# An attention-and-MLP kernel on one core: a planner's order is replaced by a fixed table, with the first weights and the first layer's pieces laid out anew

## The chip, the cores and the metric

The kernel runs on one core of a Trainium2 chip. The metric is the device time of one launch in microseconds (us). One core has five engines that run their own instruction streams in order: TensorE (PE, matmuls), VectorE (DVE), ScalarE (ACT), GpSimd (POOL) and SyncE (SP, which here only issues transfers). ACT and POOL issue transfers too.

## The reference

```python
# q, k, v: (4 batches, 8 heads, 768 steps, 64), f32
gamma = 1.0 - 2.0 ** (-5.0 - np.arange(H))
for t in range(S):
    state = gamma * state + einsum('bhd,bhe->bhde', k[:, :, t], v[:, :, t])
    y[:, :, t] = scale * einsum('bhd,bhde->bhe', q[:, :, t], state)
x = y.transpose(0, 2, 1, 3).reshape(3072, 512)
h = x @ w_in                       # 512 -> 2048
g = 0.5 * h * (1 + tanh(c * (h + 0.044715 * h**3)))
out = g @ w_out                    # 2048 -> 512
```

A linear attention with a decay for each head gives x, and a two-layer MLP with a tanh-gelu follows. All matmuls run in f16 with f32 sums.

## The kernel before

**Tiling.** The 768 steps are cut into six chunks c = 0 to 5 of 128 steps. A chunk has 4 batches of 128 steps, which are 512 tokens for the MLP. For each chunk and batch the attention does these steps on PE, with a helper for each (lines of the kernel before, and behind the slash those of the kernel after):

- T (`mm_T`, L211/L268): 8 transposes turn q and k (f16) into `qkT`. From chunk 3 on q is transposed in another way and T has 4 matmuls.
- A (`mm_A`, L220/L277): 16 matmuls on 64x64 tiles of the array, the products of k and q inside the chunk. DVE multiplies them by the decay mask (`ev_A1`, two evictions of 0.68 us for a batch).
- yc (`mm_yc`, L239/L296): the part of y from the state of earlier chunks, two batches at a time, on 64x64 tiles.
- Y (`mm_yi`, L251/L308): 8 matmuls on 128x64 tiles, the part of y from inside the chunk. The eviction gives x of this batch in f16.
- S (`mm_s`, L262/L319): 8 matmuls on 128x64 tiles for a batch, the update of the state.

The MLP's first layer is M1, its second M2. Chunk 0 and 1 have M1 as plain matmuls (`moe1_mm`, L357/L414), chunk 0 has M2 so (`m2_mm`, L515). All other chunks have both layers as 7 products of half-size blocks (`m1w_mm`, L492; `m2w_mm`, L504), whose sums DVE and POOL form (`tt`, L394) and whose results ACT (`copy_on`, L159) and DVE collect from PSUM in `st` and `o` tiles.

**Transfers.** A row is one of q, k, v of one chunk and batch, 256 KB of f32. The rows of chunk 0 are issued on SP and ACT. The weights come in 8 blocks of 512 KB, `w_in` 0 to 3 (`load_w_in`, L338) and `w_out` 0 to 3 (`load_w_out`, L347), issued on POOL. A cast on POOL, DVE or ACT makes f16 of each row (`cast`, L176 with a scale, L159 or L161 plain).

**Order.** All instructions are issued in the order in which the program emits them; each engine then runs its own in that order and waits for what it needs. Chunk 0 is written out by hand (L531 to L601): `spin(n)` puts n matmuls on zeros where PE would wait (32 in all), T, A, Y and S of the four batches follow one another, M1 of chunk 0 begins with `moe1_two` on feature pairs 0 to 2 in pieces of 256 and 128 tokens, and goes on with `moe1` for the features 6 to 15, 512 tokens wide. On POOL the casts of k and q of batches 2 and 3 stand between the issues of the weights:

```python
    load_w_in(0)
    prep1(PO, "k", 0, 2)
    for i in range(1, 4):
        load_w_in(i)
    prep1(PO, "k", 0, 3)
    prep1(PO, "q", 0, 3)
    for i in range(NO):
        load_w_out(i)
```

The loads of chunk 1 are held back by a one-element copy on ACT behind a gelu of chunk 0 (L608). Everything else, M2 of chunk 0 included, is ordered by a list scheduler while the program is built. It has a cost for each kind of step and engine (`KIND`), times at which engines, buffers and transfers come free, four threads of PE work, and takes the unit that can start first. Its units for PE keep pairs together: A of two batches, yc with both Y, S of two batches.

Of the kernel before, what the change touches and what calls it, by code (L numbers as in the profile page):

```python
# [12 lines left out]
ALU = mybir.AluOpType  # L13


@with_exitstack
def kernel(
# [9 lines left out]
    nc = tc.nc  # L27
    B, H, S, Dh = q.shape
# [92 lines left out]
    load1(nc.sync, "k", 0, 2)  # L121
    load1(nc.sync, "q", 0, 3)
    load1(nc.sync, "v", 0, 3)

# [7 lines left out]
    def spin(n):  # L132
        ps = bank("h", shape=(128, 512), name="spin_ps")
        for _ in range(n):
            nc.tensor.matmul(
                out=ps, lhsT=zero[:, 0:128], rhs=zero, start=True, stop=True
            )
# [180 lines left out]
    def o_S(b, tag="att"):  # L318
        pss["S", b] = bank(tag, shape=(128, NHP, 64), name="s_ps")  # L319
        mm_s(0, b, pss["S", b])  # L320

    def o_evS(b, eng=nc.vector):
        copy_on(eng, st_of(b), pss.pop(("S", b)))


# [48 lines left out]

    def moe1(c, fc):
        h_ps = bank("h", shape=(128, B * C), name="h_ps")
        moe1_mm(c, fc, h_ps, 0, B * C)
        gelu(g_tile(c, fc)[:, fc % 2], h_ps)

    def moe1_two(c, fp, t0, t1):  # L380

        h_ps = bank("h", shape=(128, 2, B * C // 2), name="h_ps")
        for r in range(2):
            moe1_mm(c, 2 * fp + r, h_ps[:, r, 0:t1 - t0], t0, t1)
        gelu(g_tile(c, 2 * fp)[:, :, t0:t1], h_ps[:, :, 0:t1 - t0])
# [145 lines left out]
    load1(AC, "q", 0, 2)  # L531
    load1(AC, "v", 0, 2)
# [6 lines left out]
    load1(AC, "k", 0, 3)  # L539
# [10 lines left out]
    o_S(0, "o")  # L550
    o_evY(0, AC)
    prep1(VE, "q", 0, 2)

    load_w_in(0)
    prep1(PO, "k", 0, 2)
    for i in range(1, 4):
        load_w_in(i)
    prep1(PO, "k", 0, 3)
    prep1(PO, "q", 0, 3)
    for i in range(NO):  # L560
        load_w_out(i)
    o_A(1)
    o_evA(1)
    spin(3)
    o_T(2)
    o_evT(2, AC)
    spin(2)
    o_Y(1)
    o_S(1, "o")
    o_evY(1, AC)  # L570
    prep1(AC, "v", 0, 2)
    spin(2)
    o_A(2)
    o_evA(2)
    o_evS(0, AC)
    prep1(AC, "v", 0, 3)
    o_evS(1, AC)
    spin(6)
    o_T(3)
    o_evT(3)  # L580


    t01, t2, t3 = (0, half), (half, half + C), (half + C, 2 * half)
    moe1_two(0, 0, *t01)
    o_A(3)
    o_evA(3)
    o_Y(2)
    o_S(2)
    o_evY(2, AC)
    moe1_two(0, 1, *t01)  # L590
    o_evS(2)
    moe1_two(0, 0, *t2)
    moe1_two(0, 1, *t2)
    o_Y(3)
    o_S(3)
    o_evY(3)
    o_evS(3)
    moe1_two(0, 2, *t01)
    for fp in range(2):
        moe1_two(0, fp, *t3)  # L600
    moe1_two(0, 2, half, 2 * half)  # L601

    raw["q", 1, 0] = tile_of(*LD1[0], shape=SIZE["ld"][1])
    ld_at["q", 1, 0] = LD1.pop(0)
    for fc in range(6, NF):
        moe1(0, fc)
        if fc == 12:
            nc.scalar.copy(out=raw["q", 1, 0][0:1, 0, 0:1], in_=g_tile(0, 10)[0:1, 0, 0:1])  # L608
    for bs in ((0, 1), (2, 3)):
        for b in bs:  # L610
            load1(SY, "q", 1, b)
            load1(SY, "k", 1, b)
        for b in bs:
            load1(SY, "v", 1, b)
    nc.sync.dma_start(out=dec.rearrange("p h t -> p (h t)"), in_=dec_h.ap())

    ENG = {"ACT": AC, "DVE": VE, "POOL": PO, "SP": SY}
    KIND = {
        "gelu": {"ACT": (0.51, 0.60)},
        "snap": {"ACT": (0.51, 0.59)},  # L620
        "add": {"DVE": (0.62, 0.70)},
        "evA": {"DVE": (0.61, 0.69)},
        "evY": {"DVE": (0.61, 0.69)},
        "evY1": {"ACT": (0.51, 0.59), "DVE": (0.61, 0.69)},
        "evS": {"DVE": (1.10, 1.20)},
        "evT": {"DVE": (0.62, 0.69), "ACT": (0.92, 1.01)},
        "cast": {"ACT": (0.53, 0.62), "POOL": (0.58, 0.62)},
        "cast2": {"ACT": (1.06, 1.15), "POOL": (1.18, 1.22)},
        "trq": {"DVE": (0.60, 0.69)},
        "evTk": {"DVE": (0.36, 0.44), "ACT": (0.50, 0.58)},  # L630
        "loadq": {"SP": (8.6, 0.0)},
        "scale": {"POOL": (1.00, 1.05), "DVE": (0.68, 0.75)},
        "scale1": {"POOL": (1.00, 1.05), "DVE": (0.68, 0.75)},
        "sumg": {"POOL": (1.12, 1.16), "DVE": (0.35, 0.42)},
        "sumx": {"POOL": (1.12, 1.16)},
        "sumw": {"DVE": (0.35, 0.42)},
        "sume": {"POOL": (1.12, 1.16), "DVE": (0.35, 0.42)},
        "load": {"SP": (0.90, 0.0)},
        "store": {"SP": (0.80, 0.0)},
    }  # L640
    LAT_PE, LAT, SAFE, AHEAD = 0.28, 0.07, 1.5, 0.4
    tok, T = {}, {}
    slots = {p: [0.0] * n for p, (n, _, _) in SIZE.items()}
    slots["bank"] = [0.0] * 8
    held_by = {}
    free_at = {"PE": 34.2, "ACT": 34.7, "DVE": 25.0, "POOL": 21.0, "SP": 47.5}
    landed = [48.6, 49.6, 51.5, 52.4]
    port = [0.0]
    todo, by_need = [], {}

    class Op:
        def __init__(self, kind, emit, needs, gives, alloc=(), free=(), slack=1.0, early=(), kb=0):
            self.kind, self.emit, self.needs, self.gives = kind, emit, needs, gives
            self.alloc, self.free, self.slack, self.early, self.kb = alloc, free, slack, early, kb

    def shared(o, e):

        return e == "POOL" or e == "DVE" and o.kind[:3] in ("sum", "sca")

    def op(*a, **k):  # L660
        todo.append(Op(*a, **k))

    def when(needs):
        t = 0.0
        for n in needs:
            if n not in tok:
                return None
            t = max(t, tok[n])
        return t

    def room(alloc):

        t, seen = 0.0, {}
        for off, (key, *_) in alloc:
            seen.setdefault(key[0], []).append(off)
        for p, offs in seen.items():
            at = sorted(x for x in slots[p] if x is not None)
            if len(at) < len(offs):
                return None
            t = max(t, max(a - o for a, o in zip(at, sorted(offs))))  # L680
        return t

    def take(alloc):
        for key, readers, *shape in alloc:
            p = key[0]
            i = min((x, i) for i, x in enumerate(slots[p]) if x is not None)[1]
            if p == "lq" and key[2] in BLK:
                i = key[3]
            slots[p][i] = None
            held_by[key] = [p, i, readers, 0.0]  # L690
            T[key] = bank_tile(i, *shape) if p == "bank" else tile_of(p, i)

    def give_back(keys, t):
        for key in keys:
            h = held_by[key]
            h[2] -= 1
            h[3] = max(h[3], t)
            if h[2] == 0:
                slots[h[0]][h[1]] = h[3]

    def finish_op(o, e, s):
        busy, lat = KIND[o.kind][e]
        free_at[e] = s + busy
        end = s + lat + LAT
        if shared(o, e):
            port[0] = s + busy
        if e == "SP":
            begin = max(landed[-1], s + 1.3)
            landed.append(max(begin + 1.15 * o.kb / 256, s + busy + 1.8 if o.kind == "loadq" else 0.0))
            end = landed[-1] + SAFE  # L710
            free_at[e] = max(free_at[e], landed[-4] if o.kind == "load" else 0.0)
        take(o.alloc)
        o.emit(ENG[e])
        for n in o.early:
            tok[n] = s
        for n in o.gives:
            tok[n] = end
        give_back(o.free, end)


    def ld_key(c, b, nm):
        early = c == 2 and b < 2 and nm != "v" or c in BLK and nm == "q"
        return ("lq" if early else "ld", nm, c, b)

    def q_cast(c, b):
        key = ("qk16", c, b)

        def emit(eng):
# [8 lines left out]
           alloc=[(key, 2 if c + 1 == NCk else 3)], early=[("al", key)], free=[("lq", "q", c, b)], slack=2.0)  # L737

        def tr(eng):
# [7 lines left out]
           early=[("al", "qkT", c, b)], free=[key], slack=1.5)  # L747

    def q_load(c):
# [3 lines left out]
        def emit(eng):  # L753
# [8 lines left out]
           early=[("issued", key)], slack=3.0, kb=1024)  # L762
        prev[0] = ("issued", key)

    def cast_in(c, b, nm):
# [4 lines left out]
        ldk = ld_key(c, b, nm) if c > 1 else ("ld", nm, c, b)  # L770
# [8 lines left out]
        if nm == "v":  # L779
            kind = "cast" if c < 2 else "scale"  # L780
        elif kind == "scale":
            kind = "scale1"
# [7 lines left out]
            slack=8.0 if nm == "v" else 2.0,  # L790
        )

    prev = [None]

    def load_in(c, b, nm):
# [3 lines left out]
        def emit(eng):  # L799
            eng.dma_start(  # L800
                out=T[ldk], in_=srcs[nm][b, :, c * C:(c + 1) * C, :].rearrange("h p d -> p h d")
            )

        op("load", emit, [prev[0]] if prev[0] else [], [key], alloc=[(ldk, 1)],
           early=[("issued", key)], slack=3.0, kb=256)
        prev[0] = ("issued", key)

    def sub(cost, emit, needs=(), gives=(), alloc=(), free=()):
# [504 lines left out]
```

## Time and profile before

| | |
|---|---|
| median of 3 runs | 204.56 us (204.36 to 206.03) |
| the profiled execution | 204.52 us |
| its span, first to last instruction | 202.7 us |
| mean granted TensorE clock | 0.998 |
| PE busy | 192.5 us, 95% of the span, 2376 matmuls |
| DVE / ACT / POOL busy | 150.5 / 126.6 / 96.6 us |
| DMA moved | 30.1 MB |
| first M1 matmul of chunk 0 | 17.87 us |
| last matmul ends, last store lands | 199.69, 201.83 us |

A line of a timeline gives start, duration, engine, line, operation, the tiles out<-in, their shapes, the count, and in brackets the idle time before it with what ended it. A line of the waits gives total us, times, and the longest. In a table of windows each engine has its busy us and, in brackets, its instructions; then follow the granted clock, the DMA share and GB/s.

### The profile page before, as it was taken

The numbers are of one execution on the slowest core, as the hardware profiler recorded it, in microseconds if no ns is written. First come the engines' busy times: TensorE is split into PE (matmuls) and PEld (weight loads), VectorE is DVE, ScalarE is ACT, GpSimd is POOL, SyncE is SP. The second block draws the span as 40 slices with busy tenths as digits, with TensorE's granted clock in tenths as the row PEclk, the third lists the DMA queues.
The fourth block names the chain that finished last, engine by engine and source line by source line (L and its number), as shares of the span: only waits on it lengthen the run. The fifth ranks groups of instructions, "written<-read, shape, count | busy, mean of one in ns | idle before, by whom it ended". The sixth has DMA issues, their size and how long they took to land. (4 is left out here: it accounts for less than half of the span.)

```text
span 202.7 us, 5761 instructions
## 1 busy us (share of the span) xinstructions
PE 192.5 (95%) x2376; PEld 153.1 (76%) x2376; DVE 150.5 (74%) x283; ACT 126.6 (62%) x235; POOL 96.6 (48%) x96
## 2 busy tenths in 40 slices
PE   7769999999999997999999999999999999999993
PEld 3336744455898885889889878789888888888883
DVE  4435585739787998997799998799995793297720
ACT  2482466053589547749948849948859916499421
POOL 0697000011202876852999903498914799241400
PEclk9999999999999999999999999999999999999999
DMA  7999999989998799968990669990002300020205
GB/s 165 287 263 206 209 204 218 224 196 247 206 229 169 116 251 217 224 109 152 250 254 12 117 98 188 228 259 2 3 0 84 127 3 3 0 103 25 83 4 204
DMA packets 95898, 30.10 MB, mean 148 GB/s; under 512 B 88320, under 2 KB 92800, under 8 KB 95872
## 3 DMA queue, kind: packets, MB, share of 16 engines
q1 hardware_dynamic: 85120, 23.45, 49.7%
q0 software_dynamic: 4224, 4.19, 12.5%
q10 hardware_dynamic: 6528, 2.10, 4.1%
q8 instruction: 18, 0.29, 0.6%
q14 instruction: 8, 0.07, 0.1%
HBM read 27.64 MB, written 6.29 MB: 167 GB/s over the span
## 5 line engine op out<-in xcount | busy, mean ns | idle before, releaser
L394 DVE TENSOR_TENSOR st<-ps,st 128x512 f32<-128x512 f32 x48 | 31.3, 681 | 9.4 <-PE ps L492 3.6
L504 PEld LDWEIGHTS <-s_g 128*128 128x128 f16 x320 | 30.8, 98 | 5.1 <-DVE s_g L394 0.8
L159 ACT COPY st<-ps 128x512 f32<-128x512 f32 x48 | 26.4, 602 | 13.0 <-PE ps L492 12.8
L373 ACT ACTIVATE g<-st 128x512 f16<-128x512 f32 x48 | 29.9, 649 | 7.3 <-DVE st L394 7.3
L492 PEld LDWEIGHTS <-w_in 128*128 128x128 f16 x256 | 24.7, 98 | 3.9 <-issue 0.6
L271 DVE TENSOR_TENSOR a<-ps,mask 128x512 f16<-128x512 f32 x40 | 24.8, 680 | 3.3 <-PE ps L220 3.3
L357 PEld LDWEIGHTS <-w_in 128*128 128x128 f16 x232 | 20.8, 98 | 7.7 <-issue 0.7
L394 POOL TENSOR_TENSOR s_g<-g 128x512 f16<-128x512 f16 x17 | 19.9, 1184 | 13.9 <-ACT g L373 13.9
L394 POOL TENSOR_TENSOR s_g<-g,s_g 128x512 f16<-128x512 f16 x15 | 17.8, 1191 | 16.2 <-DVE s_g L394 16.1
L159 ACT COPY o<-ps 128x512 f32<-128x512 f32 (+1 forms) x28 | 14.8, 529 | 17.0 <-PE ps L504 14.1
L504 PEld LDWEIGHTS <-g 128*128 128x128 f16 x240 | 23.1, 98 | 3.0
L373 ACT ACTIVATE g<-ps 128x512 f16<-128x512 f32 x32 | 19.3, 602 | 5.6 <-PE ps L357 5.4
L492 PEld LDWEIGHTS <-u_w 128*128 128x128 f16 x192 | 18.5, 98 | 3.0 <-issue 0.6
L504 PE MATMUL ps<-t_w,s_g 128*128 128x256 f16 x160 | 18.9, 273 | 1.2 <-ACT o L159 0.7
L504 PE MATMUL ps<-w_out,s_g 128*128 128x256 f16 x160 | 19.6, 273 | 0.0
L504 PE MATMUL ps<-w_out,g 128*128 128x256 f16 x160 | 19.3, 273 | 0.0
L492 PE MATMUL ps<-xs,w_in 128*128 128x256 f16 x128 | 18.6, 273 | 0.4 <-DVE st L394 0.4
L394 POOL TENSOR_TENSOR s_g<-s_g,g 128x512 f16<-128x512 f16 x10 | 11.9, 1187 | 14.8 <-DVE s_g L394 14.7
L394 DVE TENSOR_TENSOR o<-ps,o 128x512 f32<-128x512 f32 (+1 forms) x18 | 10.7, 593 | 9.6 <-PE ps L504 9.6
L492 PE MATMUL ps<-xs,u_w 128*128 128x256 f16 x128 | 16.6, 273 | 0.5 <-DVE a L271 0.5
L492 PE MATMUL ps<-x,w_in 128*128 128x256 f16 x128 | 16.3, 273 | 0.0
L357 PE MATMUL ps<-x,w_in 128*128 128x256 f16 x128 | 15.3, 273 | 0.1
(73 smaller groups left out, 320.6 us busy)
## 6 DMA issues: line engine op xcount, KB each, us to landing
ld<-in_v_dram SPq DMA_DIRECT2D x19, 256.0 KB, 4.4
ld<-in_k_dram SPq DMA_DIRECT2D x17, 256.0 KB, 5.3
out_dram<-o SPq DMA_DIRECT2D x8, 512.0 KB, 3.8
ldq<-in_q_dram SPq DMA_DIRECT2D x48, 64.0 KB, 2.8
w_in<-in_moe_w_in_dram POOLq DMA_DIRECT2D x4, 512.0 KB, 9.4
w_out<-in_moe_w_out_dram POOLq DMA_DIRECT2D x4, 512.0 KB, 14.4
ld<-in_q_dram SPq DMA_DIRECT2D x5, 256.0 KB, 4.6
out_dram<-o SPq DMA_DIRECT2D x5, 256.0 KB, 3.0
```

Of the source, the lines that this page charges most:

```text
L159: eng.copy(out=out, in_=in_)
L271: eng.tensor_tensor(out=a_sb[c, b, j], in0=ps, in1=mask[:, j], op=ALU.mult)
L357: nc.tensor.matmul(out=out, lhsT=w_in_sb[wi][:, kc, wr * 128:(wr + 1) * 128], rhs=xT[c][:, kc, t0:t1], start=(kc == 0), stop=(kc == NHP - ...
L373: nc.scalar.activation(out=out, in_=in_, func=AF.Gelu_apprx_tanh, scale=1.0)
L394: eng.tensor_tensor(out=out, in0=in0, in1=in1, op=op)
L492: nc.tensor.matmul(out=ps[:, f], lhsT=m1_lhs(lk, kc, 2 * g + f), rhs=x[:, kc], start=(n in FIRST and kc == 0 and f == 0), stop=(n in (1, 5 ...
L504: nc.tensor.matmul(out=ps, lhsT=m2_lhs(c, lk, fp, a), rhs=m2_rhs(rk, fp), start=(first and fp == 0), stop=(n in (1, 5, 6) and fp == NP - 1 ...
```

## The change

The planner and the written-out order of chunk 0 behind Y of batch 1 are taken out. In their place stands `ORDER`, a table of some 950 words. A word is an engine's letter (p PE, a ACT, v DVE, g POOL, s SP) and an item's number; w2 means 2 spins. The items are the same small steps as before, and the program emits them in the order of the table. With it come these changes:

- A and Y are items of one batch each, so the table can set them apart; S of chunk 0 is an item for each batch, with its eviction on ACT.
- `w_in` part 0 is issued on POOL behind a one-element copy from q of batch 0, before the casts of k; part 1 follows the casts of k of batches 0 and 1. The table then begins with the issues of `w_in` 2, 3 and `w_out` 0, 1, 2 (g0 to g4), then the casts of v of batches 2 and 3 on POOL (g9, g12), then `w_out` 3 (g5) and a one-element copy (g6, `hold`) behind which SP's loads of chunk 1 may start.
- The casts of q and k of batches 2 and 3 are on DVE, those of v on POOL. The rows of batches 2 and 3 are issued on SP, but for q of batch 2, which ACT issues.
- M1 of chunk 0 has 24 pieces: 8 feature pairs for batches 0 and 1 (256 tokens), for batch 2 (128) and for batch 3 (128). M2 of chunk 0 waits for the pieces that it reads.
- The load of the decay table `dec` goes behind q and k of chunk 2.
- The spins are 14, 3, 2, 3, 5 by hand and twice 2 in the table: 31.

```diff
+ORDER = """
+v7 p180 v8 g0 w2 p192 p170 g1 g2 g3 g4 g9 g12 g5 g6 v169 s13 s14 s15 s16 v10 p194 p186 a179
+a191 p173 v171 p182 a193 a181 w2 p196 s17 g27 s18 s19 v172 s20 s21 g30 s22 p184 s23 s24 a195
...
+"""
...
-    load1(nc.sync, "k", 0, 2)
-    load1(nc.sync, "q", 0, 3)
-    load1(nc.sync, "v", 0, 3)
+    load1(nc.scalar, "q", 0, 2)
+    for at in (("k", 2), ("v", 2), ("q", 3), ("k", 3), ("v", 3)):
+        load1(nc.sync, at[0], 0, at[1])
...
+    nc.gpsimd.tensor_copy(out=w_in_sb[0][0:1, 0, 0:1], in_=raw["q", 0, 0][0:1, 0, 0:1])
+    load_w_in(0)
     spin(14)
...
     o_Y(0)
-    o_S(0, "o")
     o_evY(0, AC)
...
+    def m1_first():
+        for t0, t1, bs, cost, kind in ((0, half, (0, 1), 0.873, "gelu"), (half, half + C, (2,), 0.45, "gelu2"),
+                                       (half + C, 2 * half, (3,), 0.45, "gelu2")):
+            for fp in range(NP):
...
+                def emit(fp=fp, t0=t0, t1=t1, key=key):
+                    for r in range(2):
+                        moe1_mm(0, 2 * fp + r, T[key][:, r, 0:t1 - t0], t0, t1)
...
+    for b in range(2):
+        tok["x", 0, b] = (12.0, 14.2)[b]
...
+            tok[key] = ((10.4, 13.9, 14.9), (15.8, 19.4, 20.4))[b - 2][i]
...
+    load_w_in(1)
+    for n in range(2, 8):
+        trig("win" if n < 4 else "wout", n % 4, n)
+    hold()
...
+    for at, word in enumerate(ORDER.split()):
+        e, i = word[0], int(word[1:])
+        if e == "w":
+            ps = bank_tile(min(x for x in slots["bank"] if x is not None)[1], (128, 512), name="spin_ps")
+            spin_on(ps, i)
+            continue
+        o = items.pop(i)
+        take(o.alloc)
+        o.emit(by[e])
...
+        give_back(o.free, 1000.0 + at)
```

`trig` issues one block of weights, each after the one before it. The numbers in `tok` are times at which rows are taken to have landed (q, k, v of batch 2: 10.4, 13.9, 14.9; of batch 3: 15.8, 19.4, 20.4). In this program they order nothing; the table alone does.

The order on PE behind Y of batch 1 begins: S of batch 0, 2 spins, M1 of batches 0 and 1 on feature pair 0, T of batch 2, M1 pair 1, S and A of batch 2 and S of batch 1, 2 spins, M1 pair 2, Y of batch 2, M1 pair 3, T of batch 3, M1 of batch 2 on pairs 0 to 2, S of batch 3, M1 of batch 2 on pair 3, A of batch 3, then M1 from pair 4 on.

## The prediction

> **What bounds the kernel now.** I read the windows of busy time first, to see where TensorE (PE) is not full, then PE's waits, then PE's timeline at the head, then the queues of POOL and SP there. The profiled execution took 204.52 us (span 202.7, so 1.8 lie outside it), 0.04 under the median of 204.56; all sums are made against 204.5.
>
> ```profile
> core 0: us, PE busy (x) PEld busy (x) DVE busy (x) ACT busy (x) POOL busy (x), PEclk, DMA share, GB/s
> 5.00:10.00 5.00, 3.80 (x45) 1.83 (x45) 2.10 (x4) 1.98 (x3) 3.16 (x3) 1.00 1.27 287
> 10.00:15.00 5.00, 3.22 (x62) 2.05 (x61) 1.76 (x3) 4.30 (x9) 4.43 (x6) 1.00 1.28 265
> 15.00:20.00 5.00, 4.80 (x75) 2.98 (x74) 2.67 (x5) 1.30 (x4) 3.88 (x5) 1.00 1.24 207
> 20.00:25.00 5.00, 4.52 (x67) 3.94 (x65) 2.97 (x9) 2.58 (x7) 0.00 (x0) 1.00 1.24 206
> 25.00:30.00 5.00, 5.00 (x28) 2.46 (x27) 4.29 (x12) 3.18 (x7) 0.00 (x0) 1.00 1.24 206
> 70.00:80.00 10.00, 9.16 (x132) 7.74 (x130) 9.14 (x14) 5.84 (x11) 7.04 (x8) 1.00 0.91 224
> 80.00:90.00 10.00, 9.49 (x117) 8.34 (x118) 10.00 (x22) 6.95 (x13) 7.84 (x8) 1.00 0.88 179
> ```
>
> PE is the bound: from 25 us on, nearly every window is full. Only 50–60, 70–90, 110–120 and 130–140 show idle time, 0.11, 0.84, 0.51, 0.47 and 0.42, together 2.35 us. At the head, DMA is as full as it gets until 35 us (share above 1.2), and PE waits or spins. Its waits by releaser:
>
> ```profile
> PE s_ps L262 <- ACT st L159: 1.6, 1, 1.6
> PE a_ps L220 <- ACT qkT L159: 0.8, 2, 0.6
> PE ps L504 <- ACT o L159: 0.7, 1, 0.7
> PE ps L504 <- DVE s_g L394: 0.5, 1, 0.5
> ```
>
> From PE's first spin (1.19) to its last matmul (199.69) are 198.5 us. 6.0 are idle (3.65 at the head, 2.35 later). 1.55 are lost in the first 14 spins, which take 4.57 us where 14 x 0.216 would do. When I add up every group of matmuls at the closest spacing that the trace has for its kind (512 columns 216 ns, 256 columns 109, 128 columns 56, and the costs of a change of tile shape, below), I get 187.2. The 3.7 left over are waits too short to be shown as idle, since a pipelined matmul still counts as busy.
>
> **The change, part by part.**
>
> *Fragments: +3.7.* The timeline prices one change between whole-array matmuls (T, M1, M2) and groups on small tiles (A, yc, Y, S):
>
> ```profile
> 14.61 0.32 PE L262 MATMUL s_ps<-v,qk 128*64 128x64 f16 x8 [1.60 <-ACT st L159]
> 17.87 1.05 PE L357 MATMUL h_ps<-x,w_in 128*128 128x256 f16 x8 [0.20 <-DMA w_in<-in_moe_w_in_dram]
> 18.84 0.42 PE L220 MATMUL a_ps<-qkT 64*64 64x128 f16 x16
> 19.19 0.41 PE L251 MATMUL y_ps<-a,v 128*64 128x128 f16 x8
> 44.57 0.64 PE L220 MATMUL ps<-qkT 64*64 64x128 f16 x32
> 45.14 3.63 PE L515 MATMUL ps<-w_out,g 128*128 128x512 f16 x16
> ```
>
> A of one batch, 16 matmuls, takes 0.35 from start to start (18.84 to 19.19); a pair of batches, 32 matmuls, 0.57 (44.57 to 45.14): a pair cut in two costs 0.13 more. The reason stands in the single starts: the last matmul of a small group takes 129 to 151 ns to the next start instead of some 50, and the last whole-array matmul ahead of A or yc 202 instead of 109, ahead of Y or S 149. The order of the new program has 23 groups of A in place of 14, 24 of Y in place of 14, 11 of S in place of 8; exits from small groups go from 34 to 58, entries from 21 to 43. 24 exits x 0.10 = 2.4; 22 entries, half at 0.093 and half at 0.040 = 1.5; transposes in more places +0.2; one spin and some small turns −0.4. Sum +3.7 (bounds 2.5 and 4.5). It falls on PE, so nothing covers it.
>
> *Head: −1.0.* w_in part 0 is issued when q of batch 0 has landed (about 4) instead of at 9.01, so M1 can start near 13 to 14 instead of 17.87. In before, 12.60 to 24.14 hold 2.3 us of waits (1.60, 0.20, 0.24, 0.24) and 8 spins (1.7): 4.0 to win. After keeps 4 spins there (0.9), and I leave it 1.3 of waits, because x of batches 0 and 1 and the rows of batch 2 come about when M1 wants them. It also comes there with less done: T of batch 2 and S of batch 0, which before had behind it at 12.6, take 0.45 + 0.25. 4.0 − 2.2 − 0.7 = 1.1; taken −1.0, bounds 0 and −2.4.
>
> *Later waits: −3.5.* A table laid out with each group where its operands are ready can win at most what there is: 2.35 of idle and 3.7 of short waits. I take the idle and a third of the rest; bounds 0 and −6.0.
>
> *At nothing.* Casts of q and k of batches 2 and 3 go from POOL (1.05 each) to DVE (0.68): DVE is busy 4.4 of the 10 us from 10 to 20. If it were full, 0.7 would stand ahead of each T. M1 of chunk 0 has 24 gelus, 16 of them of 256 columns (0.38), where before had 18, 14 of them of 512 (0.60): ACT +1.0 us, under M1 and M2, where it is busy 7.5 of 20 us (30 to 50). The 128-column matmuls cost half of the 256-column ones. The loads of chunk 1 are released behind w_out part 3 instead of by a gelu at 32.4; DMA has the same bytes to move and no gap, so they land from 36 us on as before, under some 28 us of M1 and M2.
>
> *Rows of batch 3: 0 to +7.5.* This decides. After issues w_in part 1 on POOL at about 9.1, then parts 2, 3 and w_out 0, 1, 2 back to back, and w_out 3 behind the casts of v. Before, they went out with casts between them:
>
> ```profile
> 9.01 0.94 POOL L338 DMA_DIRECT2D w_in<-in_moe_w_in_dram  x1
> 11.56 2.29 POOL L338 DMA_DIRECT2D w_in<-in_moe_w_in_dram  x3
> 13.85 2.07 POOL L176 TENSOR_TENSOR qk<-ld,cst 128x512 f16<-128x512 f32 x2
> 15.84 3.04 POOL L347 DMA_DIRECT2D w_out<-in_moe_w_out_dram  x4
> ```
>
> ```profile
> 5.89 1.76 SPq L108 DMA_DIRECT2D ld<-in_q_dram  x1
> 7.70 1.76 SPq L108 DMA_DIRECT2D ld<-in_v_dram  x1
> ```
>
> A row block of 256 KB takes 0.905 us of a full DMA (landings 9.59, 10.49 ... 14.13), a block of weights 2.53 (17.82 is the first, then 19.92, 22.44, 24.97). SP cannot issue far ahead: an issue with two rows outstanding takes 1.76, and the last row, issued by 9.46, landed at 14.13, 4.7 later. With w_in 0 and 1 in front, k and v of batch 3 would land at 19.4 and 20.4 (the table's own times, 13.2 and 14.1 plus two blocks), so SP issues them at about 13.6 to 15.7. POOL's blocks 2, 3 and w_out 0 are issued from 10 to 12.7, ahead of that. Which goes first? w_in 0 of before, issued by 9.95, moved no packet until 13.2, when the rows, all issued by 9.46, were as good as in. Either blocks are served in the order of issue, or a block of POOL's becomes active some 3.3 us after its issue; the trace holds both.
>
> PE executes in order. Work ahead of T of batch 3 ends at about 20.2, and T needs k + 0.73 (DMA to cast, DVE cast); S of batch 3 comes 1.8 of PE work later and needs v + 0.6. If a block is active 3.3 us after its issue, w_in 2 (14.1) comes ahead of v and perhaps of k: k lands at 21.9, T starts at 22.6, a stall of 2.4; with only v behind it 1.5, and with w_in 3 ahead of v as well 4.1. I take +2.3.
>
> The Trainium skill ("DMA: Bandwidth & Descriptors", section "Queues, rings and completion order") says that each DMA engine takes turns between the queue rows it has work for, packet by packet. By that rule POOL's queue would get half, batch 3 would land near the table's 19 to 20, and the sum would be 203.7, the first rival. The row of w_in 0, silent for 3.3 us beside two busy queues, is against turns from the moment of issue.
>
> Sum: 204.5 + 3.7 − 1.0 − 3.5 + 2.3 = **206.0**.
>
> **Rivals.**
> 1. *Batch 3 lands as the table has it.* No stall: 203.7, with the bounds of the other terms 202 to 205.5. For it: two queues shared DMA evenly in order of issue in before. Against it: SP's rows are issued late and POOL's blocks early.
> 2. *Strictly by order of issue: slower.* w_in 2, 3 and w_out 0 go ahead of k of batch 3: 3 x 2.53 = 7.6 later, 27.0; T at 27.7, a stall of 7.5 at 20 us. 203.7 + 7.5 = 211.2. It decides as soon as three POOL blocks are served ahead of k. For it: all 15 early transfers of before landed in the order of their issue. Against it: the 3.3 us of silence of w_in 0 could be a start-up that puts POOL's blocks back by as much. The clock is 1.00 in all these windows; a cold one cost 1.55 over the first spins, so a stall that long could add that much, to 212.7. The Trainium skill ("TensorE: Matmul & The Clock Gate", Part 1) puts the fall to half speed at about 3.4 us of idling; no stall of before is that long.
> 3. *The table doesn't run as laid out:* M1 starts no earlier or the later waits only move. Then the fragments remain: 204.5 + 3.7 − 0.5 − 0.5 = 207.2. For it: DVE is busy 9 to 10 of 10 us from 70 to 90, and a fixed order can't bend around a late sum.
>
> **How the numbers follow.** Forecast 0.40, rival 1 0.33, rival 2 0.20, rival 3 0.07. A measurement of this kernel can tell about 1% from no change, 202.5 to 206.6. Faster: a third of rival 1 and a little of the forecast, 0.14. Slower: rivals 2 and 3 and two fifths of the forecast, 0.42. Same: the rest, 0.44. The range 202.0 to 212.0 holds the forecast's own 203.5 to 208, rival 1 and most of rival 2.
>
> **What would show it.** Right: M1's first matmul at 13 to 14.5; a wait of 1.5 to 4 us of PE on DMA or a cast ahead of T or S of batch 3 (L268, L319 of after) at 20 to 24, and weights' packets among the rows' by then; A of 16 matmuls and Y of 8 between M1 groups at 0.35 to 0.45 each; later windows fuller, with more matmul records. Wrong: no wait above 0.5 at 19 to 24 (rival 1), one of over 5 (rival 2), or idle windows from 50 on as before (rival 3). If PE's busy time falls instead of rising, the fragments were mis-sized.

## The result, and the profile after

The changed kernel takes 220.37 us (median of 4 runs, 218.19 to 221.01), the kernel before 204.49: a ratio of 1.0739, interval 1.0646 to 1.0833. The profiled execution took 220.89 us, with a span of 219.1 and a mean granted clock of 0.958. The prediction, 206.0 within 202 to 212, was wrong: the kernel is slower by 15.9 us, and the slowest rival stood at 211.2 to 212.7. Ratios leave out executions over 1.5% above the fastest of their kernel, one of before_w0 (211.04) and the profiled one of hybrid (208.96).

The windows of busy time after (columns as before: window, PE, PEld, DVE, ACT, POOL, clock, DMA share, GB/s):

```profile
20.00:25.00 5.00, 0.23 (x3) 0.11 (x2) 1.46 (x3) 0.60 (x1) 0.00 (x0) 0.83 1.22 196
25.00:30.00 5.00, 3.04 (x20) 1.91 (x20) 0.44 (x1) 1.46 (x3) 0.00 (x0) 0.50 1.22 196
30.00:35.00 5.00, 3.17 (x28) 3.03 (x29) 2.39 (x5) 0.00 (x0) 0.00 (x0) 0.50 0.89 146
35.00:40.00 5.00, 3.91 (x46) 3.17 (x46) 1.90 (x5) 1.32 (x4) 1.47 (x3) 0.50 0.54 76
80.00:90.00 10.00, 10.00 (x191) 7.83 (x190) 8.47 (x15) 5.76 (x11) 4.12 (x4) 1.00 0.89 185
```

From 20 to 40 us PE is half idle, and from 25 on its clock is at half. Behind that, the windows are fuller than before: 0.21 us of idle time from 40 us on, where before had 2.35. PE's timeline shows where the hole is, and DVE's what the first wait rests on:

```profile
14.46 1.03 PE L406 MATMUL ps<-x,w_in 128*128 128x256 f16 x8 [0.15 <-PE spin_ps L192]
24.89 0.32 PE L308 MATMUL ps<-a,v 128*64 128x128 f16 x1 [4.77 <-DVE a L328]
30.87 0.61 PE L268 MATMUL ps<-iden,qk 128*128 128x128 f16 x4 [2.55 <-DVE qk L233]
36.09 0.42 PE L319 MATMUL ps<-v,qk 128*64 128x64 f16 x8 [2.05 <-POOL v L218]
23.55 0.69 DVE L233 TENSOR_TENSOR qk<-ld,cst 128x512 f16<-128x512 f32 x1 [6.88 <-DMA ld<-in_q_dram]
```

M1 does begin 3.4 us earlier (14.46 for 17.87). Then Y of batch 2, T of batch 3 and S of batch 3 wait one after another. The first wait names DVE's mask, but DVE itself sat for 6.88 us in front of the cast of q of batch 3, which stands ahead of the mask and waited for its row. The chain of work that ended last puts the whole stretch on one transfer (start, duration, what):

```profile
9.50 3.57 SPq L164
13.11 22.26 DMA ld<-in_v_dram
38.05 4.74 PE ps L406 x40
```

The row v of batch 3, issued from 13.11, landed at 35.37. Rows and weights landed in this order: w_in 0 13.5, v of batch 2 16.9, w_in 1 17.3, w_in 2 21.8, q of batch 3 23.5, w_in 3 25.1, w_out 0 28.5, k of batch 3 30.1, w_out 1 31.8, w_out 2 35.2, v 35.4. That is neither the order of issue nor the table's: q of batch 3, whose issue ended at 9.45, came behind w_in 2, whose issue began at 9.62. The queues' records tell why. From 18 to 30 us, before and after (queue: packets, MB, share of 16 engines):

```profile
q0 software_dynamic: 2481, 2.46, 123.6%
```

```profile
q0 software_dynamic: 1869, 1.86, 91.4%
q1 hardware_dynamic: 1872, 0.47, 29.9%
```

In before, POOL's queue q0 has this time for itself. In after, q0 and SP's queue q1 move the same number of packets, 1869 and 1872. But a packet of weights has 1024 bytes and one of a row 256, so rows get a fifth of the bytes.

### The profile page after: what moved, and what is told of

Same layout as the page of the kernel before. It is cut to its first block, busy times and chain, and to the rows that moved or that the text cites. A ratio compares the mean times of both kernels' runs of the same rounds, so it can differ in the third digit from the quotient of the medians.

```text
span 219.1 us, 5922 instructions
## 1 busy us (share of the span) xinstructions
PE 203.0 (93%) x2463; PEld 160.5 (73%) x2463; DVE 148.1 (68%) x278; ACT 119.8 (55%) x228; POOL 110.2 (50%) x115
## 4 chain that ended last, share of the span: by engine, by line
PE 80%; DMA 10%; SPq 5%; DVE 2%; issue 0%; POOL 0%; ACT 0%; DVEq 0%
PE ps L541 28%; PE ps L529 22%; PE ps L406 12%; DMA ld<-in_v_dram 10%; PE ps L552 6%; SPq L164 5%; PE ps L277 3%; PE ps L308 3%; PE ps L268 3%; PE ps L319 1%; PE ps L296 1%; DVE v L233 1%; DVE st L431 1%; DVE s_g L431 1%; POOL v L218 0%
## 5 line engine op out<-in xcount | busy, mean ns | idle before, releaser
L422 ACT ACTIVATE g<-ps 128x512 f16<-128x512 f32 (+1 forms) x56 | 28.4, 540 | 28.3 <-PE ps L406 22.4
L328 DVE TENSOR_TENSOR a<-ps,mask 128x512 f16<-128x512 f32 x44 | 28.5, 680 | 16.8 <-PE ps L277 16.6
L431 POOL TENSOR_TENSOR s_g<-g 128x512 f16<-128x512 f16 x23 | 27.3, 1196 | 18.4 <-ACT g L422 18.4
L406 PE MATMUL ps<-x,w_in 128*128 128x256 f16 (+1 forms) x320 | 35.0, 270 | 0.2 <-PE spin_ps L192 0.2
L216 ACT COPY st<-ps 128x512 f32<-128x512 f32 x48 | 26.5, 588 | 14.7 <-PE ps L529 14.6
L406 PEld LDWEIGHTS <-w_in 128*128 128x128 f16 x320 | 27.8, 106 | 5.2 <-issue 1.3
L529 PEld LDWEIGHTS <-w_in 128*128 128x128 f16 x256 | 24.0, 98 | 3.5
L216 ACT COPY o<-ps 128x512 f32<-128x512 f32 (+1 forms) x28 | 14.4, 527 | 14.2 <-PE ps L541 13.9
L431 POOL TENSOR_TENSOR s_g<-s_g,g 128x512 f16<-128x512 f16 x12 | 14.1, 1177 | 13.7 <-DVE s_g L431 13.4
L529 PEld LDWEIGHTS <-u_w 128*128 128x128 f16 x192 | 18.1, 98 | 2.5 <-DVE o L431 0.2
L541 PE MATMUL ps<-w_out,s_g 128*128 128x256 f16 x160 | 19.4, 273 | 0.2 <-DVE s_g L431 0.2
L218 POOL CAST v<-ld 128x512 f16<-128x512 f32 x4 | 3.0, 741 | 33.0 <-DMA ld<-in_v_dram 33.0
L541 PE MATMUL ps<-t_w,s_g 128*128 128x256 f16 x160 | 19.4, 273 | 0.0
L529 PE MATMUL ps<-xs,u_w 128*128 128x256 f16 x128 | 18.1, 273 | 0.0
L529 PE MATMUL ps<-x,w_in 128*128 128x256 f16 x128 | 18.0, 273 | 0.0
L233 POOL TENSOR_TENSOR v<-ld,cst 128x512 f16<-128x512 f32 x15 | 15.8, 1065 | 0.5 <-DMA ld<-in_v_dram 0.4
## 6 DMA issues: line engine op xcount, KB each, us to landing
w_in<-in_moe_w_in_dram POOLq DMA_DIRECT2D x4, 512.0 KB, 10.3
```

What stands on the lines that cost most here:

```text
L216: eng.copy(out=out, in_=in_)
L233: eng.tensor_tensor(out=o, in0=heads(src, sw), in1=heads(cst[:, col:col + H].unsqueeze(2), sw).broadcast_to([128, NHP, 2, Dh]), op=ALU.mult,)
L328: eng.tensor_tensor(out=a_sb[c, b, j], in0=ps, in1=mask[:, j], op=ALU.mult)
L406: nc.tensor.matmul(out=out, lhsT=w_in_sb[wi][:, kc, wr * 128:(wr + 1) * 128], rhs=xT[c][:, kc, t0:t1], start=(kc == 0), stop=(kc == NHP - ...
L422: nc.scalar.activation(out=out, in_=in_, func=AF.Gelu_apprx_tanh, scale=1.0)
L431: eng.tensor_tensor(out=out, in0=in0, in1=in1, op=op)
```

## The experiments

My theory after this trace, called turns below: queues with work take packets in turn, so small packets lose, and the row of v of batch 3 sets the hole. The rivals: service in order of issue, the clock, DVE's order, and the fragments.

**v2_first.** The weights from w_in 2 on go behind the cast of v of batch 2.

```diff
-v7 p180 v8 g0 w2 p192 p170 g1 g2 g3 g4 g9 g12 g5 g6
+v7 p180 v8 g9 g0 w2 p192 p170 g1 g2 g3 g4 g12 g5 g6
```

> The cast of v of batch 2 goes ahead of the issues of w_in 2, 3 and w_out 0 to 2 on POOL (they then go out at about 17.5 us instead of 9.6). Turns (my theory: POOL's queue and SP's queue take turns packet by packet, 1024 bytes against 256, so that rows get a fifth of the bytes while weights are queued): with w_in 1 done at about 17.3 and the next block starting some 3.3 us after its issue, q, k, v of batch 3 land at full speed by about 20.5 instead of 23.5, 30.1 and 35.4; no wait of PE above 1 us from 15 to 25; clock 1.00; total 206 (fragments +3.9, head -0.5, later waits -1.6 against 204.5). Rival (the cold clock and the stalls come from DVE's queue, where the cast of q of batch 3 stands ahead of the masks of batch 2): gain of at most 5 us, 215 or more.

Measured 207.73 us, ratio 1.0118 (1.0080 to 1.0157); 206 was expected. The rows of batch 3 landed at 17.9, 18.9 and 21.0, and behind the wait for the first spins (1.2, as in before) none above 0.8 us is left:

```profile
PE spin_ps L192 <- DVE zero L182: 1.2, 1, 1.2
PE ps L529 <- ACT st L216: 0.8, 1, 0.8
```

The place of one word in the table is worth (1.0739 − 1.0118) x 204.5 = 12.7 us, of the 15.1 that the ratio 1.0739 makes of the loss. Gains against the changed kernel are worked out so, from the ratios, from here on. The edit cures the loss under several theories; the next ones tell them apart.

**w0_late.** `load_w_in(0)` and its gate go from the head to just ahead of `load_w_in(1)`.

```diff
-    nc.gpsimd.tensor_copy(out=w_in_sb[0][0:1, 0, 0:1], in_=raw["q", 0, 0][0:1, 0, 0:1])
-    load_w_in(0)
...
+    load_w_in(0)
     load_w_in(1)
```

> w_in 0 is issued behind the casts of k of batches 0 and 1, directly before w_in 1 (8.8 instead of 4.9); all else as in the changed kernel, the early issues of w_in 2 to w_out 2 too. Turns: POOL's queue moves no packet before about 13, so all rows but the last are in by then; v of batch 3 lands at 14.5 to 17.5; the stalls of batch 3 go; PE waits some 2.5 us for w_in 0 at 14 to 17; total 206.5 to 208.5. Rival (transfers are served in the order of their issue): v of batch 3, whose issue ends at about 13, stands behind w_in 0 to 3 and lands at 24 or later, PE stalls until then; total 212 or more.

Measured 214.94, ratio 1.0470 (1.0430 to 1.0509): my numbers missed and the rival's held. k and v of batch 3 landed at 22.5 and 29.1. But the landings are not in the order of issue: k (from 9.50) came behind w_in 1 (from 9.89, at 20.3), v (from 10.37) behind w_in 2 and 3 (from 10.63 and 11.37, at 23.0 and 26.4). The records show turns, 1:1 from 15 us on; what I had wrong is when a row starts. Row k, issued by 10.3, moved nearly nothing from 12 to 14 and then ran beside w_in 1 in full. The waits (the second on the cast of v):

```profile
15.84 1.05 PE L406 MATMUL ps<-x,w_in 128*128 128x256 f16 x8 [1.82 <-DMA w_in<-in_moe_w_in_dram]
29.86 0.42 PE L319 MATMUL ps<-v,qk 128*64 128x64 f16 x8 [4.86 <-POOL v L218]
```

So the early w_in 0 is not the whole of it: without it 5.5 us come back, two waits for w_in 0 and 1 of 2.6 included, and 9.6 of the 15.1 stay. Most of the hole is made by weights that are on POOL's queue before the last rows.

**half_packets.** Each block as two transfers of 256 columns, here for w_in; w_out is split alike.

```diff
-        nc.gpsimd.dma_start(
-            out=w_in_sb[i],
...
+        for r in range(2):
+            n0 = w_in_at[i] * 128 + r * 256
+            nc.gpsimd.dma_start(
+                out=w_in_sb[i][:, :, r * 256:r * 256 + 256],
```

> Each block of weights goes as two transfers of 256 columns, packets of 512 bytes instead of 1024; order of issues as in the changed kernel. Turns by packet: rows get a third of the bytes instead of a fifth while both queues are busy, a row takes some 4.2 us instead of 6.6, v of batch 3 lands at about 27 instead of 35.4; total 6 to 8 us below the changed kernel, about 213. Rival (queues share by bytes or by order of issue, packet size doesn't matter): rows land as before within 1 us, total within 2 us of the changed kernel.

Measured 215.64, ratio 1.0516 (1.0455 to 1.0576), 4.6 us below the changed kernel where 6 to 8 were expected, with v of batch 3 at 29.3 instead of 35.4 (27 expected). From 17 to 27 us:

```profile
q0 software_dynamic: 2433, 1.21, 87.4%
q1 hardware_dynamic: 2433, 0.61, 46.5%
```

The counts are equal again and rows have a third of the bytes. The size of the other queue's packets sets a row's share; order of issue, which was not touched, would have changed nothing. The time is a less clean test than the landing, since the edit makes a stall of its own: the issues of w_out held POOL up to 24.5, so that the cast of v of batch 2, landed at 15.8, came late:

```profile
25.18 0.43 PE L319 MATMUL ps<-v,qk 128*64 128x64 f16 x8 [7.66 <-POOL v L218]
```

**two_queues.** v of batch 2 and k of batch 3 are issued on ACT.

```diff
-    for at in (("k", 2), ("v", 2), ("q", 3), ("k", 3), ("v", 3)):
+    for at in (("k", 2), ("q", 3), ("v", 3)):
         load1(nc.sync, at[0], 0, at[1])
...
+    load1(AC, "v", 0, 2)
     spin(14)
...
     o_evT(0, AC)
+    load1(AC, "k", 0, 3)
```

> The changed kernel, with v of batch 2 and k of batch 3 issued on ACT as in the kernel before, so that the rows still to come stand on two queues. Turns (my theory): rows get two packets of three, 512 of 1536 bytes instead of 256 of 1280, and v of batch 3 lands at 27 to 31 instead of 35.4; 4 to 6 us faster than the changed kernel. Rival (POOL's weights are served first because they were issued first, whatever the rows' queues): v of batch 3 lands at 34 or later, total within 2 us of the changed kernel.

Measured 212.70, ratio 1.0378 (1.0340 to 1.0416), 7.4 us below the changed kernel; v landed at 27.8. From 15 to 20 us three queues share by turns:

```profile
q0 software_dynamic: 683, 0.68, 80.3%
q1 hardware_dynamic: 684, 0.17, 26.2%
q10 hardware_dynamic: 628, 0.16, 14.3%
```

The gain exceeds the 4 to 6 expected; v landed 7.6 us earlier than in the changed kernel, as much as the gain. Turns between queues are shown.

**warm.** Spins in front of the three waits.

```diff
-... s22 p184 ... a197 p175 ... p212 p190
+... s22 w20 p184 ... a197 w19 p175 ... p212 w15 p190
```

> 54 spins more in front of Y of batch 2 (20), T of batch 3 (19) and S of batch 3 (15), where PE waited, so that the clock stays at full speed. Landing-bound (my theory: until S of batch 3, at 36 us, the landing of v at 35.4 sets the time, so only what the half clock cost after it comes back): 2 to 2.5 us faster than the changed kernel, 218. Rival (the half clock from 23 to 40 us costs about half of its stretch that PE worked): 5 us or more faster, 215.5 or less.

Measured 219.27, ratio 1.0678 (1.0620 to 1.0735), 1.2 us below the changed kernel, at a clock of 0.999. The intervals overlap, so the 1.2 is not clear of noise, and 2 to 2.5 were expected; the last spins ended at 36.92 where the cast of v ended at 36.17, so they took some 0.8 back. The rival's 5 us or more is ruled out. The half clock is not a loss of its own until the last row has landed: whatever PE does faster before, it waits out at S of batch 3.

**dve_order.** The cast of q of batch 3 (v10) behind the masks of batch 2 (v171, v172).

```diff
-... s16 v10 p194 ... a195 v11 ...
+... s16 p194 ... a195 v10 v11 ...
```

> The changed kernel, with the cast of q of batch 3 on DVE behind the two masks of batch 2 instead of ahead of them. Landing-bound (my theory): the wait of 4.8 us ahead of Y of batch 2 goes, but T and S of batch 3 still wait for k (30 us) and v (35 us), so the end moves by less than 1 us. Rival (DVE's order is what costs the time): 4 us or more faster than the changed kernel.

Measured 220.37, ratio 1.0799 (1.0778 to 1.0821): no gain, as expected. The wait moved from Y to T:

```profile
PE ps L268 <- DVE qk L233: 10.1, 2, 6.2
```

**v3_first.** As v2_first, but g9 and g12 both ahead of g0.

```diff
-v7 p180 v8 g0 w2 p192 p170 g1 g2 g3 g4 g9 g12 g5 g6
+v7 p180 v8 g9 g12 g0 w2 p192 p170 g1 g2 g3 g4 g5 g6
```

> As v2_first, but with the cast of v of batch 3 ahead of the weights' issues too, so that they go out at about 20.5 us. A block of POOL's has started 3.3 us after its issue so far: w_in 2 lands at about 27, M1 of pair 4 wants it at 24.1, PE waits 3 us; total 3 us above v2_first, 210.5. Rival (a block starts at once when the queue is free): w_in 2 lands at 24 and the total is within 1 us of v2_first.

Measured 211.42, ratio 1.0345 (1.0332 to 1.0358), 210.5 expected: w_in 2, issued from 21.45, landed at 27.56 and PE waited 3.5 us for it. Between an issue that is just early enough for M1 (16.5 in v2_first) and one that is too late lie less than 5 us.

**before_w0.** The kernel before, with w_in 0 alone issued early.

```diff
     load1(AC, "v", 0, 2)
+    nc.gpsimd.tensor_copy(out=w_in_sb[0][0:1, 0, 0:1], in_=raw["q", 0, 0][0:1, 0, 0:1])
+    load_w_in(0)
     spin(14)
...
-    load_w_in(0)
     prep1(PO, "k", 0, 2)
```

> The kernel before with one part of the change alone: w_in 0 is issued on POOL behind a one-element copy from q of batch 0, at about 5 us instead of 9. Turns: while w_in 0 moves (about 9 to 13.5 us), POOL's, SP's and ACT's queues take packets in turn, so rows get a third of the bytes; v of batch 3 lands at about 16.5 instead of 14.1, T of batch 3 starts 0.3 to 1.0 us later, and since PE's written order has M1 behind it, M1 can't use the early weights: 0.3 to 1.0 us slower than before. Rival (early weights cost the rows nothing): M1 no longer waits for w_in, 0.2 us faster or the same.

Measured 209.63, ratio 1.0221 (1.0179 to 1.0263): the sign was right and the size far off. v of batch 3 landed at 18.1, but it was k of batch 2 that decided. It landed at 13.7 instead of 10.5, and its cast is on POOL, with all further weights queued behind it:

```profile
13.73 1.04 POOL L176 TENSOR_TENSOR qk<-ld,cst 128x512 f16<-128x512 f32 x1 [4.43 <-DMA ld<-in_k_dram]
14.71 2.30 POOL L338 DMA_DIRECT2D w_in<-in_moe_w_in_dram  x3
```

w_in 1 to 3 left 3.2 us later than in before (14.71 for 11.56), and T of batch 2 waited 2.4 us. Behind that wait the clock stood at 0.50 for 6.8 us (16.75 to 23.58): the same work from the two spins behind T of batch 2 to the first M1 takes 7.8 us (15.06 to 22.89) where before takes 5.8 (12.07 to 17.87). The wait and the half clock together are most of the 5 us by which M1 starts later.

**before_singles.** The kernel before, with A, Y and S as units of one batch.

```diff
-        units.append([A(0, 0.35), A(1, 0.33)])
+        units += [[A(0, 0.35)], [A(1, 0.35)]]
...
-            units.append([yc((0, 1)), A(2, 0.23), A(3, 0.23), yi(0, 0.33), yi(1, 0.33)])
+            units += [[yc((0, 1)), yi(0, 0.33)], [A(2, 0.35)], [yi(1, 0.33)], [A(3, 0.35)]]
```

> The kernel before with one part of the change alone: its planner gets A, Y and S of chunks 1 to 5 as units of one batch instead of pairs, which in its order makes 23 groups of A, 23 of Y and 10 of S (14, 14 and 8 before) and 42 changes from whole-array work to small tiles instead of 21, about as the changed kernel has (23, 24, 11 and 43). Rows, weights and chunk 0 are untouched. Fragments (my theory): 21 more entries and exits at some 0.17 each, 3 to 4 us slower than before. Rival (the small groups run beside other work at no cost, and v2_first and hybrid lost their time to DMA): within 1 us of before.

Measured 215.59, ratio 1.0544 (1.0498 to 1.0590), 11 us. The expectation named the fragments alone, and the run has more. In its profile M2 of chunk 0 starts as before (34.23 for 34.09). From 40 us on PE's idle time grows from 2.35 to 5.51, and one wait of 2.06 us is followed by 16 matmuls at half speed, which cost 1.7. The last matmul ends 10.3 later than before's (210.00 for 199.68); less 3.2 of idle time and these 1.7, 5.4 are left for the small groups, with waits too short to show. So the fragments are as dear as I priced them or dearer, and a planner that was set for pairs loses about as much again in waits.

**hybrid.** The table of v2_first for chunk 0, then before's own order, with its pairs, written down as table words.

```diff
-... (the words of v2_first behind M1 of chunk 0)
+... (the planner's sequence of the kernel before: M2 of chunk 0, chunks 1 to 5)
```

> The table of v2_first for chunk 0 (attention and M1), then the order of the kernel before for everything else (M2 of chunk 0 and chunks 1 to 5, with A, Y and S in pairs), as a table. Fragments (my theory: the single groups of A, Y and S in the later chunks cost about 3.5 us, and the table's order wins 0.7 there): 2.5 to 3 us faster than v2_first, 0.5 us below before. Rival (v2_first is slower than before by what the early weights do to chunk 0 and to the rows of chunk 1): within 1 us of v2_first.

Measured 205.40, ratio 1.0049 (1.0019 to 1.0079): 1.4 us below v2_first, half of what I expected. In its profiled execution, at 208.96 the longest of the seven, v of batch 3 landed at 26.5, behind w_in 2, and S waited 3.6 us; how often its other executions lose that race, the trace can't say. So I tried two ways to decide that race.

**hybrid_two_queues** and **hybrid_gate.** The first takes the edit of two_queues; the second lets w_in 2 wait for q of batch 3:

```diff
+        def emit(eng):
+            if n == 2:
+                eng.tensor_copy(out=w_in_sb[2][0:1, 0, 0:1], in_=T["ld", "q", 0, 3][0:1, 0, 0:1])
+            load(i)
```

> hybrid, with v of batch 2 and k of batch 3 issued on ACT. In the profiled execution of hybrid v of batch 3 landed at 26.5 because w_in 2, issued at 15.3 behind the cast of v of batch 2, had started before it; PE waited 3.6 us there. With two queues all rows are in by about 19: no wait of PE above 1 us from 15 to 30, 0.5 to 1.5 us faster than hybrid, 203.5 to 204.5. If chunk 0 gains nothing by early weights, it stays at hybrid's 205.

> hybrid, with a one-element copy on POOL from q of batch 3 ahead of the issue of w_in 2, so that w_in 2 goes out at about 18.5 and starts at about 22. v of batch 3 lands at 20.5 in every execution; M1 of pair 4 waits for w_in 2 (25 instead of 24.1) about 1 us. Total 204 to 205.2: the lost races of hybrid are gone, part of it is paid to the later weights.

Measured 206.88 (1.0107, 1.0066 to 1.0148) and 207.62 (1.0129, 1.0094 to 1.0163): both missed, and neither is better than hybrid. v of batch 3 landed at 20.7 in both, as wanted, but the first k of chunk 1 at 41.0 and 42.1, where before has 37.2, and T of chunk 1 waited:

```profile
42.79 0.40 PE L276 MATMUL ps<-iden,qk 128*128 128x128 f16 x4 [1.04 <-DVE qk L241]
```

Turns cost more than order. From 18 to 30 us after moved 1869 packets of weights, 0.753 of what before moved with q0 alone (2481), and 1872 of rows, 0.136 of what rows alone make in 12 us (9148 in the 8 us from 4 to 12 of before, so 13,722): 0.89 together. A ninth of DMA's time is lost there, and before mixes rows and weights hardly at all. It is not all that makes the rows of chunk 1 late: between the last row and w_in 2, DMA moved 30 GB/s from 19.4 to 20.8 in hybrid_two_queues and 21 GB/s from 19.4 to 22.0 in hybrid_gate. How the lateness divides between the two is not shown. No version beat the kernel before.

## Why the prediction was wrong

- **Rows of batch 3, +2.3 (0 to +7.5): this step failed.** I let k and v wait for a block or two and then land at full speed, k at 21.9. In after k landed at 30.1 and v at 35.4, since from 14 us on rows and weights took turns packet by packet and rows had a fifth of the bytes. From M1 on pair 2 to the 48 matmuls of M1 behind Y of batch 3, after takes 24.0 us (19.09 to 43.07) and v2_first, for the same matmuls, 9.7 (18.37 to 28.06): the hole costs 14.3, the half clock in it included. I had read "order of issue" out of w_in 0, which moved nothing beside the rows until 13.3, and had set aside the Trainium skill's sentence on turns by packet ("DMA: Bandwidth & Descriptors", "Queues, rings and completion order"). The runs bear it out, 1869 to 1872, 2433 to 2433, 683 to 684. And I read it as half of the bandwidth, where it says packets: at 1024 bytes to 256, a fifth. My first rival rested on that half and fell with it.
- **What spoke for order of issue** held for rows alone: the 15 early transfers of before landed in the order in which their issues ended, with w_in 0 last. It did not carry over to rows that have weights beside them (q of batch 3 and w_in 2, above). And the silence of w_in 0 is only in part a start-up: from the start of an issue to the first packet are 4.3 us in before and 4.6 in after, but 1.45 for w_in 2 in v3_first, where no row moved any more. Why it takes longer beside rows is open.
- **Casts on DVE, at nothing:** I priced them by how busy DVE is, and not by the row that a cast waits for. Hence the first stall, 4.8 us ahead of Y of batch 2, stood in no term. By dve_order it cost nothing of its own, since T and S wait for later rows.
- **Rival 2** had the place and the sign right (211.2), with the wrong mechanism and less than half the size: 6.7 of 15.9 us. Its point on the clock held: 0.50 from 25 to 40. By warm that was worth 1.2 us, an estimated 2 without the spins that ran too long; 1.55 was foreseen.
- **Fragments, +3.7:** under-sized. Without the hole (v2_first against before, profiled executions) PE's busy time grows by 6.2, of which 1.1 is a slower run of the first 14 spins (5.72 for 4.57) and 5.1 are fragments, with what short waits may stand among them. The slower spins are not the change's doing: before_singles, whose head is before's own, has 5.86. One error stands in the rows: Y entered from a 256-column matmul costs 203 ns, as A does. The 149 of before stood behind a 128-column matmul (56), so each entry costs 93 ns more, and 22 of them 2.0 instead of 1.5. By the counts of the groups the exits grow to 58 from 36, not from 34, which takes 0.2 back.
- **Head, −1.0:** in v2_first PE's idle time before 40 us is 1.29 where before has 3.66, 2.4 less, of which the slower first spins cover 1.1. Near enough; M1 began at 14.46 in after, within the 13 to 14.5.
- **Later waits, −3.5:** over-sized. Idle time from 40 us on fell by 1.4 in v2_first and by 2.1 in after; whether the short waits that I counted on went, busy time does not show. 5.1 + 1.1 − 2.4 − 1.4 = 2.4 is by how much the last matmul of v2_first ends later than before's (202.13 for 199.68). With the hole, and 0.7 less of later waits, 2.4 + 14.3 − 0.7 = 16.0; after's last matmul ends 16.1 later (215.75).

## What to carry to other kernels

Before a transfer is moved earlier, ask which queues have work at that moment and how large their packets are: a queue of 256-byte packets beside one of 1024 got a fifth here, and the row that came last set the time, whatever the table said. Late landings spread through in-order engines: a cast that waits holds what stands behind it (DVE's masks in after, POOL's weights in before_w0), so the engine named in a wait is often not the cause. Cutting pairs of small-tile groups has a price on PE that is read from two rows, and it needs a gain of that size elsewhere.

## What the runs showed of the hardware

- From 14 us on packets were dealt in equal numbers between the queues that had packets ready, also between three, and whatever their size (the rows above); whether a turn is one packet or several, equal numbers don't tell. Mixing 256 and 1024 bytes lost 11% of what each queue moves alone.
- A queue with rows issued does not always move them. From 10 to 12 us of after q0 moved 357 packets and q1 157, and row k of w0_late moved nearly nothing for 2 us after the row ahead of it had ended. Why is open.
- A block issued on POOL landed 5.4 to 6.1 us after its issue began when its queue had nothing else (hybrid_two_queues 18.54 to 23.92, v3_first 21.45 to 27.56), of which 2.5 are transfer. Its first packet came after 1.45 there, after 2.4 in v2_first and after 4.6 in after, beside rows.
- An issue on SP can take long while its queue is held up: 6.88 us for v of batch 3, where before's took 1.76.
- The clock fell after shorter waits than the some 3.4 us of idling that the Trainium skill gives ("TensorE: Matmul & The Clock Gate", Part 1). In before_singles, after 2.06 us of waiting and 4 matmuls at full speed, 8 matmuls of 256 columns took 1.92 us instead of 1.04, and in two_queues, after waits of 2.89 and 0.29, 1.89. After a wait of 1.82 (w0_late) they took 1.05.
